# A second chunk in seven products instead of sixteen plain steps, with the weight rounding taken off GpSimd

## The chip, the cores and the metric

The kernel runs on one core of a Trainium2 chip. The metric is the device time of one execution in microseconds (us). A core has engines that run side by side, each with its own queue that it works through in order: TensorE (PE in the profile, with PEld for its weight loads), VectorE (DVE), ScalarE (ACT), GpSimd (POOL) and SyncE (SP), which issues most transfers. An engine stops at an instruction whose operands are not there yet, and everything behind it in its queue stops with it.

## The reference

Retention attention over 8 batches, 8 heads, 576 positions and 64 dimensions is followed by a feed-forward layer on 4608 tokens. All is in 32-bit floats.

```
scores = (q @ k^T) / 8 * gamma_h ** (i - j) for i >= j, else 0
x      = (scores @ v), heads side by side            # 4608 x 512
h      = x @ w_in                                    # 512 -> 2048
g      = h * erf(softplus(h))
out    = g @ w_out                                   # 2048 -> 512
```

The two weights arrive as 64-bit floats, so the kernel has to round them to 32 bits itself, from the two 32-bit words of each number.

## The kernel before

The tokens are cut into 9 chunks of 512 (number c), the 2048 inner features into 4 groups (number g). A `First(g, c)` makes the inner features of one group for one chunk, a `Second` multiplies them by w_out and adds to the output. Both are done as a two-by-two block product by Winograd's scheme: seven block products instead of eight, for which sums of the operands' blocks (and of the results) are made by VectorE. Only the first two chunks of the first group use a plain product with all eight blocks, because at that point the sums are not there.

Attention runs in pieces of 128 tokens, 36 in all, four to a chunk. Each piece has three stages. The text calls them T (bring q and k into transposed form), S (scores, with the mask multiplied in by VectorE) and O (outputs, scaled by VectorE into the x of the chunk, and the running state), each with the piece's number, so that O7 ends chunk 1. They are worked off in one fixed order, and every call of `attend` puts the next of them among the feed-forward work.

```python
    ps_at = ctx.enter_context(tc.tile_pool(name="ps_at", bufs=4, space=PSUM))   # attention's banks
    ps_a = ctx.enter_context(tc.tile_pool(name="ps_a", bufs=2, space=PSUM))
    ps_e = ctx.enter_context(tc.tile_pool(name="ps_e", bufs=1, space=PSUM))     # tags "e" and "g"
    ...
    # order of stages: T0 S0, then T(i+1) O(i) S(i+1); for i = 5 and 7: O(i) T(i+1) S(i+1)
    # from piece 8 on T has its q (from piece 12 on its k too) transposed by VectorE, in 32x32 squares
```

Rounding of one part of a weight (each group has four parts of w_in, "wa", and four of w_out, "wb") takes five steps, and each call of `round_weights(n)` puts n steps in the queues. After a group's last part the sums of its blocks follow as four more steps for wa and four for wb. They overwrite block A21 of w_in, which the plain product reads.

```python
            nc.scalar.activation(a_f, high_f, AF.Abs)                    # step 1, ScalarE
            nc.scalar.mul(out=r_f, in_=low, mul=2.0**-52)
            yield
            nc.vector.tensor_scalar(out=a_f, ... op0=ALU.max, op1=ALU.min)            # step 2
            yield
            nc.vector.tensor_scalar(out=a, ... logical_shift_left, bitwise_and)       # step 3
            yield
            nc.vector.scalar_tensor_tensor(out=a, in0=high, ...)                      # step 4
            yield
            nc.vector.tensor_scalar(out=high, in0=a, scalar1=0xFF800000, ... bitwise_and)   # step 5
            engine = nc.vector if (name, g) == ("wa", 0) else nc.gpsimd
            engine.tensor_tensor(out=r_f, in0=high_f, in1=r_f, op=ALU.mult)
            engine.tensor_tensor(out=a_f, in0=a_f, in1=r_f, op=ALU.add)
            ...
            for n in sums:
                of = (sums_in if n == "wa" else sums_out)(*(operands(n, g)[:, i] for i in range(7)))
                ...
```

The operand sums of x, made by VectorE, and the plain and the seven-product form of `First`:

```python
    def operands_x(g, c):
        ...
        if g == 0 or c < PLAIN:
            tt(t1, b12, b11, ALU.subtract)
            tt(t2, b22, t1, ALU.subtract)
            tt(b12, b22, b12, ALU.subtract)
        else:                      # what was stored in x holds b22 - b12 already
            tt(t2, b12, b11, ALU.add)
            tt(t1, b22, t2, ALU.subtract)
        if g == 0:
            store_x(c)
        tt(t4, b21, t2, ALU.subtract)

        def plain(self):           # 16 steps of two matmuls of 256 columns
            for dc in range(n_dc):
                for n in range(4):
                    for j in range(GP):
                        nc.tensor.matmul(acc[n][...], lhsT=wa[...], rhs=t[:, dc, ...], ...)
                    if dc == n_dc - 1:
                        nc.scalar.copy(out=(self.t2 if tok else self.t1)[:, f], in_=acc[n])
                    yield

        # first(), middle(), last(): 7 steps, each one block product of four matmuls of 256 columns
        def first(self):
            self.product(A11, self.a, True);  nc.scalar.copy(out=self.t1[:, 0], in_=self.a);  yield
            self.product(A12, e, True);  tt(self.t1[:, 0], e, self.t1[:, 0], ALU.add);  yield
        def middle(self):
            self.product(S2, self.a, False);  nc.scalar.copy(out=self.t1[:, 1], in_=self.a);  yield
            self.product(S3, self.e, True);  yield
            self.product(S1, self.a, False);  nc.scalar.copy(out=self.t2[:, 1], in_=self.a)
            tt(self.t2[:, 1], self.e, self.t2[:, 1], ALU.add);  yield
        def last(self):
            self.product(S4, self.a, False);  nc.scalar.copy(out=self.t2[:, 0], in_=self.a);  yield
            self.product(A22, self.e, False);  tt(self.t1[:, 1], self.e, self.t1[:, 1], ALU.add)
            self.softplus();  yield
```

`multiply` forms g from h and erf; `sums` makes the operand sums of the second product, s1 and s2 (part 0), s3 and s4 (part 1). `Second.first` is the products B11 and B21, `Second.middle` T2, T3 and T1, and `Second.last` B22 and T4. T2 is added into the bank of B11, so it has to wait until ScalarE has copied B11 out of it.

The second chunk before, with the first `Second` behind it:

```python
    most[0] = before_chunk(3)
    attend(after_chunk(1))                    # O7
    store_x(1)
    for step, _ in enumerate(firsts[1].plain()):
        if step % 2 == 0:
            attend(min(done[0] + 1, most[0]))
        round_weights(int(step > 1))
        if step == 1:
            firsts[0].softplus()
            firsts[0].erf()
        elif step == 5:
            firsts[0].multiply()
        elif step == 8:
            firsts[0].sums()
    seconds[0].begin()
    run(seconds[0].first(), (2, 2))           # an attend and two rounding steps after each product
    firsts[1].softplus()
```

## Time and profile before

| | before |
|---|---|
| time, median of 3 runs | 1024.89 us (1024.43 to 1025.56) |
| span of the profiled execution | 1024.3 us |
| granted TensorE clock | 1.000 |
| DMA, mean | 162 GB/s |

The page of the profile lists for each engine its busy time and its share of the span, then groups of instructions with their mean duration in ns and the idle time ahead of them. A timeline lists instructions in order of their start, with the duration of the whole row behind the start; several alike are one row (x4). In this trace one matmul of the program is two rows[...], and eight such rows make one block product. Durations of TensorE overlap, so what an instruction really takes of the engine is read from one start to the next.

### The profile page before, as it was taken

What the parts mean: (1) busy time and instruction counts of PE and PEld (TensorE: products, weight loads), DVE (VectorE), ACT (ScalarE), POOL (GpSimd) and SP (SyncE); (2) the same over time, 40 slices, a digit from 0 to 9 for tenths busy, and PEclk for the clock granted to TensorE, in tenths of its full rate; (3) what the DMA queues carried; (4) which work ended last, traced back from release to release, by engine and by line L of the source; (5) the groups of instructions that cost most, each with busy time, mean ns of one, the idle gap of its engine ahead of it and who ended that gap; (6) DMA issues with size and microseconds to landing.
All of it is one profiled execution on the core that took longest, in us unless ns stands there. A gap on an engine that the chain in (4) does not pass through costs nothing.

```text
span 1024.3 us, 15955 instructions
## 1 busy us (share of the span) xinstructions
PE 1014.0 (99%) x6348; PEld 876.5 (86%) x6348; DVE 666.9 (65%) x1062; ACT 390.2 (38%) x481; POOL 122.0 (12%) x122
## 2 busy tenths in 40 slices
PE   8999999999999999999999999999999999999998
PEld 7788888887888888888888888888888888888887
DVE  3769777967976656656666666666567655555555
ACT  2354134233234444434343444444433333333332
POOL 2133112122312110010001001000100000000000
PEclk9999999999999999999999999999999999999999
DMA  9997989969974344544445345444433334444434
GB/s 189 214 245 163 238 194 224 251 152 253 246 188 164 110 159 145 166 160 156 163 142 164 123 147 162 165 144 144 144 124 124 123 131 127 131 136 131 126 88 119
DMA packets 146986, 165.76 MB, mean 162 GB/s; under 512 B 97376, under 2 KB 121568, under 8 KB 138848
## 3 DMA queue, kind: packets, MB, share of 16 engines
q1 hardware_dynamic: 144832, 163.57, 56.1%
q10 hardware_dynamic: 2080, 1.18, 0.5%
q8 instruction: 50, 0.82, 0.3%
q14 instruction: 24, 0.20, 0.1%
HBM read 117.52 MB, written 47.19 MB: 161 GB/s over the span
## 4 chain that ended last, share of the span: by engine, by line
PE 87%; DMA 5%; SPq 3%; DVE 2%; issue 1%; POOL 1%; ACT 0%; ACTq 0%; DVEq 0%; POOLq 0%
PE a L604 23%; PE a L496 22%; PE g L604 12%; PE g L496 11%; PE e L496 6%; PE e L604 5%; PE s L347 2%; PE o L365 2%; DMA wraw<-in_moe_w_in_dram 2%; SPq L147 2%; SPq L131 1%; PE o L388 1%; DMA raw_qs<-in_q_dram 1%; PE o L377 1%; DMA raw_ks<-in_k_dram 1%
## 5 line engine op out<-in xcount | busy, mean ns | idle before, releaser
L496 PE MATMUL a<-x,wa 128*128 128x256 f32 x1088 | 258.3, 380 | 0.0
L496 PEld LDWEIGHTS a<-x,wa 128*128 128x128 f32 x1088 | 205.7, 190 | 28.9 <-issue 0.7
L604 PE MATMUL a<-wb,s 128*128 128x256 f32 x840 | 200.0, 381 | 0.0
L604 PEld LDWEIGHTS a<-wb,s 128*128 128x128 f32 x840 | 158.4, 190 | 23.3 <-ACT o L618 0.7
L99 DVE TENSOR_TENSOR t<-g,t 128x512 f32<-128x512 f32 x68 | 46.9, 690 | 150.1 <-ACT t L526 112.6
L496 PE MATMUL g<-x,wa 128*128 128x256 f32 x544 | 129.2, 380 | 0.0
L496 PEld LDWEIGHTS g<-x,wa 128*128 128x128 f32 x544 | 102.8, 190 | 14.5 <-issue 0.2
L99 DVE TENSOR_TENSOR o<-a,o 128x512 f32<-128x512 f32 x104 | 71.5, 687 | 46.4 <-PE a L604 46.4
L521 ACT COPY t<-a 128x512 f32<-128x512 f32 x34 | 19.9, 586 | 187.8 <-PE a L496 187.8
L99 DVE TENSOR_TENSOR t<-t,s 128x1024 f32<-128x1024 f32 x72 | 88.6, 1271 | 0.0
L565 ACT ACTIVATE s<-t 128x1024 f32<-128x1024 f32 x72 | 72.1, 1048 | 29.6 <-DVE t L99 29.6
L274 POOL TENSOR_TENSOR wraw<-wraw 128x512 f32<-128x512 f32 x28 | 29.5, 1053 | 438.9 <-DVE wraw L272 178.4
L99 DVE TENSOR_TENSOR x<-x 128x512 f32<-128x512 f32 x115 | 75.7, 692 | 1.2
L532 ACT COPY t<-a 128x512 f32<-128x512 f32 x34 | 19.9, 587 | 144.0 <-PE a L496 144.0
L569 ACT ACTIVATE s<-s 128x1024 f32<-128x1024 f32 x72 | 72.1, 1048 | 0.4
L604 PE MATMUL g<-wb,s 128*128 128x256 f32 x280 | 66.7, 381 | 0.5 <-DVE t L99 0.5
L604 PE MATMUL e<-wb,t 128*128 128x256 f32 x280 | 66.6, 380 | 0.0
L604 PE MATMUL a<-wb,t 128*128 128x256 f32 x280 | 66.6, 380 | 0.0
L604 PE MATMUL g<-wb,t 128*128 128x256 f32 x280 | 66.4, 380 | 0.0
L496 PE MATMUL e<-x,wa 128*128 128x256 f32 x272 | 64.8, 381 | 0.0
L99 DVE TENSOR_TENSOR sT<-s,cst 128x512 f32<-128x512 f32 x72 | 46.2, 682 | 25.2 <-PE s L347 25.1
L99 DVE TENSOR_TENSOR o<-g,o 128x512 f32<-128x512 f32 x70 | 48.0, 685 | 21.3 <-ACT o L618 18.6
(86 smaller groups left out, 1245.4 us busy)
## 6 DMA issues: line engine op xcount, KB each, us to landing
od<-o SPq DMA_DIRECT2D x54, 512.0 KB, 3.3
x<-xd SPq DMA_DIRECT2D x27, 1024.0 KB, 4.8
o<-od SPq DMA_DIRECT2D x27, 1024.0 KB, 5.3
raw_qs<-in_q_dram SPq DMA_DIRECT2D x96, 112.0 KB, 4.5
raw_ks<-in_k_dram SPq DMA_DIRECT2D x84, 112.0 KB, 4.2
xd<-x SPq DMA_DIRECT2D x9, 1024.0 KB, 5.1
raw_v<-in_v_dram SPq DMA_DIRECT2D x64, 128.0 KB, 4.4
wraw<-in_moe_w_in_dram SPq DMA_DIRECT2D x32, 256.0 KB, 5.7
```

What stands on the lines that cost most here:

```text
L99: nc.vector.tensor_tensor(out=out, in0=in0, in1=in1, op=op)
L131: nc.sync.dma_start(out=t[part * SQ : (part + 1) * SQ, :, at : at + m - SQ], in_=tokens[:, :, d0 : d0 + m - SQ])
L147: queue.dma_start(out=t[r0 : r0 + n, e::2, :], in_=heads.rearrange("h p d -> p h d"))
L274: engine.tensor_tensor(out=r_f, in0=high_f, in1=r_f, op=ALU.mult)
L347: nc.tensor.matmul(ps[e][:, p, :], lhsT=t["kT"][heads[e], p, :], rhs=t["qT"][heads[e], p, :], start=True, stop=True)
L365: nc.tensor.matmul(o[p % 2][heads[(e + p) % 2], p // 2, :], lhsT=t["v"][:, 2 * p + e, :], rhs=t["sT"][:, e, p, :], start=(p < 2), stop=(no ...
L496: nc.tensor.matmul(acc[:, j * TH : (j + 1) * TH], lhsT=weights["wa", self.g][:, a, d, j * P : (j + 1) * P], rhs=x[self.g, self.c][a][:, d, :],
L521: nc.scalar.copy(out=self.t1[:, 1], in_=self.a)
L532: nc.scalar.copy(out=self.t2[:, 0], in_=self.a)
L565: nc.scalar.activation(self.s[:, j], t, AF.Softplus)
L569: nc.scalar.activation(self.s[:, j], self.s[:, j], AF.Erf)
L604: nc.tensor.matmul(acc[:, tp, :], lhsT=left[:, j * TH + tp * P : j * TH + (tp + 1) * P], rhs=weights["wb", self.g][:, b, j, :], start=(sta ...
```

## The change

The second chunk (c = 1) of the first group is made with seven block products too. That needs the sums of w_in before it (they move ahead of the rounding of w_out, into the first chunk's plain steps, at a point where the last plain read of A21 has been issued) and the operand sums of x for chunk 1. All of w_out's first group is rounded on VectorE, so that GpSimd has no part in it. The sums of the first chunk's activations are split in two. As chunk 1 is now stored with b22 - b12 in it, later groups take the shorter form of `operands_x` for it.

```diff
-                yield src, "wa", g, a, dc % 2, ["wa"] if g > 0 and dc == n_dc - 1 else []
+                yield src, "wa", g, a, dc % 2, ["wa"] if dc == n_dc - 1 else []
 ...
-                    sums = (["wb"] if g > 0 else ["wb", "wa"]) if (f, j) == (1, GP - 1) else []
+                    sums = ["wb"] if (f, j) == (1, GP - 1) else []
 ...
-            engine = nc.vector if (name, g) == ("wa", 0) else nc.gpsimd
+            engine = nc.vector if g == 0 else nc.gpsimd
 ...
-    PLAIN = 2
+    PLAIN = 1
 ...
-    for what in "alkakakawkakakawwaa3awa2aaa5ppppaa5wwppa5ppawappwcppa5ppaaapp5s":
+    for what in "alkakakawkakakawwaa3awa2aaa5ppppaa5wwppa5ppawappwcpp4a5ppaaapp5s":
 ...
     most[0] = before_chunk(3)
     attend(after_chunk(1))
-    store_x(1)
-    for step, _ in enumerate(firsts[1].plain()):
-        if step % 2 == 0:
+    attend(done[0] + 1)
+    operands_x(0, 1)
+    f = firsts[1]
+    for step, _ in enumerate(chain(f.first(), f.middle(), f.last())):
+        if step > 0:
             attend(min(done[0] + 1, most[0]))
-        round_weights(int(step > 1))
-        if step == 1:
+        round_weights((0, 2, 2, 2, 4, 2, 2)[step])
+        if step == 0:
             firsts[0].softplus()
             firsts[0].erf()
+        elif step == 2:
+            firsts[0].multiply()
         elif step == 5:
-            firsts[0].multiply()
-        elif step == 8:
-            firsts[0].sums()
+            firsts[0].sums((0,))
     seconds[0].begin()
-    run(seconds[0].first(), (2, 2))
-    firsts[1].softplus()
+    for step, _ in enumerate(seconds[0].first()):
+        attend(min(done[0] + 1, most[0]))
+        if step == 0:
+            firsts[0].sums((1,))
```

In the string of the first chunk, `a` is one attention stage, `p` one plain step, `w` the load of one weight part, and a digit that many rounding steps.

## The prediction

> **What bounds the kernel now.** I read the page's first part, then busy time by stretches, then the timelines of the four engines between 46 and 110 us (the change lies there), and the chain of work that ended last for the same stretch. The page first, and four stretches (start:end, length, busy time and instructions of PE, PEld, DVE, ACT and POOL, granted clock, DMA share, GB/s):
>
> ```profile
> PE 1014.0 (99%) x6348; PEld 876.5 (86%) x6348; DVE 666.9 (65%) x1062; ACT 390.2 (38%) x481; POOL 122.0 (12%) x122
> 60.88:84.00 23.12, 22.93 (x208) 18.70 (x205) 17.74 (x34) 12.28 (x16) 8.41 (x8) 1.00 0.97 232
> 84.00:99.34 15.34, 15.25 (x157) 12.48 (x155) 13.46 (x20) 9.41 (x11) 4.72 (x5) 1.00 0.82 182
> ...
> 300.00:400.00 100.00, 100.00 (x560) 86.51 (x559) 65.45 (x105) 45.02 (x59) 12.94 (x12) 1.00 0.46 158
> 400.00:500.00 100.00, 100.00 (x465) 88.04 (x464) 63.91 (x99) 42.70 (x52) 9.94 (x9) 1.00 0.43 147
> ```
>
> TensorE is the bound nearly everywhere: without a gap from 300 us on, and with 0.28 us of gaps between 60.88 and 99.34, which is the stretch that the change rewrites. So there is almost no waiting to take away there, and the gain must come from fewer matmuls. But VectorE is busy 31.2 of those 38.5 us, and the change gives it more. Its timeline where the chunk begins, and ScalarE's beside it (start, duration, line and operation, in brackets the idle time ahead and what ended it):
>
> ```profile
> 60.10 0.43 DVE L259 TENSOR_SCALAR wb<-wb 128x512 f32<-128x512 f32 x1 [1.85 <-ACT wb L254]
> 61.75 0.43 DVE L272 TENSOR_SCALAR wraw<-wb 128x512 uint32<-128x512 uint32 x1
> 62.09 0.42 DVE L99 TENSOR_TENSOR sums<-o,state 128x256 f32<-128x256 f32 x1
> 63.09 0.76 DVE L326 STREAM_TRANSPOSE qT<-raw_qs 128x256 f32<-128x256 f32 x2
> 65.54 1.29 DVE L99 TENSOR_TENSOR sT<-s,cst 128x512 f32<-128x512 f32 x2 [1.69 <-PE s L347]
> 70.34 0.43 DVE L259 TENSOR_SCALAR wb<-wb 128x512 f32<-128x512 f32 x1 [3.51 <-ACT wb L254]
> ```
>
> ```profile
> 63.14 1.28 ACT L565 ACT_TABLE_LOAD   x1
> 64.43 2.00 ACT L565 ACTIVATE s<-t 128x1024 f32<-128x1024 f32 x2
> 66.45 1.28 ACT L569 ACT_TABLE_LOAD   x1
> 67.75 2.00 ACT L569 ACTIVATE s<-s 128x1024 f32<-128x1024 f32 x2
> 69.66 0.66 ACT L254 ACTIVATE wb<-wraw 128x512 f32<-128x512 f32 x1
> ```
>
> VectorE has room until 70.34 (3.51 us of it waiting for ScalarE, which is in softplus and erf), and none after. The one real wait in the stretch is in the chain (start, us, what):
>
> ```profile
> 82.98 1.04 POOL wraw L274
> ...
> 84.10 1.62 POOL wb L275
> ...
> 85.74 1.51 DVE wb L99
> ```
>
> GpSimd's add took 1.62 us, VectorE stood still 1.18 us for it, the mask of S10 came late, and O10 lost about 0.4 us on TensorE. That is what the second part of the change is aimed at.
>
> [...]the trace has 690. In a row of independent ones the next starts 0.60 us after the last, in a dependent row 0.72. [...]here multiply 1.05 and add 1.28 to 1.62 against 0.69. [...]the first sum of chunk 0 took 1.77 us beside a GpSimd add, where the others took 0.68. [...]below I count the queues in program order.
>
> **The change part by part.** Three durations carry it: a block product (eight rows) 1.73 us from start to start, a plain step (four rows) 0.865, and 0.1 us more at each passage between attention and a product.
>
> TensorE: 16 plain steps (13.84) become 7 products (12.11): 1.73 us less, the whole direct gain. The number of attention stages is the same.
>
> VectorE, added: eight tensor_tensor for the multiply and add of four parts of w_out, 8 x 0.69 = 5.5; the operand sums of chunk 1, 4 in about 2.85; three adds of the product, 3 x 0.6 = 1.8. Sum 10.1 us. Taken away in the busy part: the four sums of w_in (3.46 from 90.21 to 95.15, where GpSimd slowed them), which now fall at 47.7 to 50.4, into a wait of 3.29 us ahead of the mask at 50.99, and so are free. The parts of w_out that come earliest are free too: part 0 ends about 55.7, ahead of O6 at 55.95. In g = 1 to 3 one tensor_tensor less each, 2 us in stretches where TensorE sets the pace: nothing.
>
> Now the walk through the queues, which decides.
>
> (a) w_out's part 1 is 1.53 us longer on VectorE (62.09 becomes 63.62), so T8's transposes end at 65.4 instead of 63.85. TensorE has O7 to 60.88, T8 to 61.37, A11 to 63.10, A12 to 64.83, then S8, which waits for T8 until 65.5: 0.7 lost.
>
> (b) The operand sums start at 65.3; the second, t2, is there at about 67.05. TensorE is through S8 at 66.6: 0.45 lost. Then S2, T9, S3 to 71.1, O8 (masks at 70) to 72.75, S1 to 74.6, S9, S4 and T10 to 77.95.
>
> (c) ScalarE's A11 copy ends at 63.85, then softplus and erf with their tables take 6.52 as before, so w_out's part 2 can go on at 71.05 on VectorE, behind a wait of 1.1. From there VectorE has, in order: clamp 0.35, T9 0.62, shift and merge 1.08, multiply of chunk 0 2.27, O8 0.66, rest of part 2 1.87, the add of S1 0.6, masks of S9 1.2, part 3 3.5, T10 0.62, two sums of w_out 1.32, s1 and s2 1.32, the add of A22 0.6. The S1 add is thus done at 78.5, the A22 add at 87.0. A22 accumulates in the bank which the S1 add reads: 78.6 instead of 77.95, 0.65 lost.
>
> (d) TensorE goes on: A22 to 80.4, O9 to 81.95, B11 to 83.8, S10 (T10 at 83.9, 0.2 lost), B21 to 86.95. T11's bank comes free with O9's scaling at 88.1: 1.2 lost.
>
> (e) ScalarE's softplus of chunk 1 stands ahead of the copy of B11 and cannot start before the A22 add, 87.0. Two activations of 1.05 each and the copy give 89.8; T2, waiting for that copy, starts there instead of 88.65: 1.15 lost.
>
> (f) From T2 on TensorE sets the pace again: T2 1.82, O10 2.08, T3 1.92, S11 1.09, T1 1.92, O11 2.08. The third chunk's first product starts at 100.7. Before, it started at 99.34.
>
> So 1.73 us of matmuls and about 0.6 of old waits are saved, and about 4.3 us of new waits come in (0.7 + 0.45 + 0.65 + 0.2 + 1.2 + 1.15): with passages that fall otherwise, **+1.4 us** at that point. Behind it VectorE has its sums of chunk 2 at about 105.5 and the masks of S12 at 107.2, where O12 wants them at 107.3, so nothing more is lost, and nothing is won back in a stretch without gaps.
>
> **The rivals.** First: VectorE is quicker than I count, because GpSimd no longer reads beside it (8.41 us of GpSimd work in 60.88 to 84.00, of which 5.2 were the rounding). For it speak the 1.77 and the 1.51 us of slowed instructions; against it, that I took undisturbed durations already. If the waits of (c) to (e) shrink by 3 us, 1.73 + 0.6 less 1.3 makes the kernel 1.0 us faster, 1023.9. Second: the backlog of VectorE is worse. GpSimd still weighs the values (1.04 each) beside the long run of (c), and each collision costs up to a microsecond, through (d) and (e) straight onto TensorE: 1.5 us more, 1027.8. Third: the shift is swallowed later, as at 232 to 252 us, where TensorE waits 1.0 and 0.5 us for transposed k behind transfers. But the chain there goes back through SyncE's queue to a VectorE instruction at 199.06 which itself followed a TensorE product at 196.48, so it moves with the rest; at most a microsecond either way.
>
> **Range and chances.** 1024.89 + 1.4 = 1026.3. As the first rival is the likelier error, I take **1026.0**. The three runs before lie 1.1 us apart, the walk may be off by 1.5, so **1023.8 to 1027.7**. Two per cent are 20 us, more than all the work of the second chunk's product: chances 0.01 faster, **0.98 within 2%**, 0.01 slower.
>
> **What would show it right or wrong.** Right: PE has eight instructions fewer; the four sums of wa lie between 47 and 51 us; no GpSimd multiply or add of wb; TensorE waits at S8, S2, A22, T11 and T2 with VectorE or ScalarE as releaser, some 4 us in all between 60 and 92; the first product of the third chunk starts near 100.7. Wrong: if it starts before 98.5, VectorE kept up and the gain of the matmuls came through; if after 102, there is a wait that I did not see, most likely behind ScalarE's softplus; and if it starts near 100.7 but the time differs from 1026 by over a microsecond, the later DMA stretch around 200 to 250 us swallowed or added time.

## The result, and the profile after

The changed kernel takes 1029.15 us (median of 6 runs, 1027.46 to 1030.04), and the kernel before, in 6 runs beside it, 1024.96 (1024.43 to 1025.94): a ratio of 1.0037, 95% interval 1.0024 to 1.0050. So it is about 4 us slower, where 1.1 was forecast. Two later sets gave 1.0044 [1.0031, 1.0056] and 1.0036 [1.0023, 1.0049].

First the page's line of busy times of the changed kernel, then the same two stretches as before (start:end, length, busy time and rows of PE, PEld, DVE, ACT and POOL, granted clock, DMA share, GB/s):

```profile
PE 1014.1 (99%) x6340; PEld 875.7 (85%) x6340; DVE 674.5 (66%) x1074; ACT 389.8 (38%) x481; POOL 113.0 (11%) x114
```

```profile
60.88:84.00 23.12, 20.93 (x185) 17.10 (x183) 22.29 (x38) 13.94 (x18) 3.95 (x4) 1.00 0.95 218
84.00:99.34 15.34, 13.41 (x114) 10.28 (x113) 10.84 (x22) 6.84 (x8) 1.61 (x2) 0.89 0.77 170
```

PE has the eight rows fewer that seven products instead of 16 plain steps leave out. But in the two stretches it now stands still 2.19 + 1.93 = 4.12 us, where it stood still 0.28, and VectorE is busy 22.29 of the first 23.12 us. The clock column of the second stretch, 0.89, was 1.00 before.

TensorE's rows of the changed kernel that had to wait, with what ended each wait in brackets, and the third chunk's first product:

```profile
64.88 1.16 PE L347 MATMUL s<-qT,kT 64*128 64x128 f32 x16 [0.53 <-DVE qT L326]
66.51 1.96 PE L496 MATMUL a<-x,wa 128*128 128x256 f32 x8 [0.47 <-DVE x L100]
...
78.86 1.99 PE L496 MATMUL g<-x,wa 128*128 128x256 f32 x8 [1.20 <-DVE t L100]
...
88.05 0.63 PE L332 MATMUL pt_k<-ident,raw_k 128*128 128x128 f32 x4 [0.76 <-PE e L604]
89.85 3.38 PE L604 MATMUL a<-wb,s 128*128 128x256 f32 x8 [1.17 <-ACT o L618]
...
102.52 1.99 PE L496 MATMUL a<-x,wa 128*128 128x256 f32 x8
```

The five with waits are S8, S2, A22, T11 and T2, in this order. The waits add up to 4.13 us. (T11's line names TensorE itself as what ended the wait, which tells nothing; it starts at 88.05, inside VectorE's scaling of O9 at 87.54 to 88.28, which frees its bank; in e3, where that ends at 85.4, T11 does not wait.) Two things were not in the forecast: A22 waits 1.20 us, and T2's eight rows, 1.99 us elsewhere, take 3.38. The engines behind A22's wait, in one timeline of GpSimd and VectorE:

```profile
72.40 1.06 POOL L313 TENSOR_TENSOR raw_v<-raw_v,cst 128x512 f32<-128x512 f32 x1 [4.54 <-DMA raw_v<-in_v_dram]
72.48 3.20 DVE L100 TENSOR_TENSOR t<-t,s 128x1024 f32<-128x1024 f32 x2
...
78.12 0.68 DVE L100 TENSOR_TENSOR t<-g,t 128x512 f32<-128x512 f32 x1
```

The multiply of chunk 0 began 0.08 us after GpSimd began to weigh values, and took 3.20 us. The same two instructions in the kernel before, from the timelines of the two engines:

```profile
72.34 2.35 DVE L99 TENSOR_TENSOR t<-t,s 128x1024 f32<-128x1024 f32 x2
...
85.67 1.04 POOL L313 TENSOR_TENSOR raw_v<-raw_v,cst 128x512 f32<-128x512 f32 x1
```

The multiply stood at the same place and took 2.35 us; the weighing came 13 us later, because it stood behind the rounding of w_out's last two parts in GpSimd's queue (75.83 to 85.7): its values had landed at 72.29, and GpSimd stood still for 4.62 us ahead of the last part's multiply (82.98), but the weighing did not pass it. With the rounding gone from that queue, the weighing starts at 72.40, 0.16 us after its values have landed (72.24), and meets the multiply. Everything behind the multiply in VectorE's queue is 0.85 us later, so the add of S1, which frees A22's bank, is too. Behind T2 stands ScalarE, in its own timeline:

```profile
87.32 2.01 ACT L565 ACTIVATE s<-t 128x1024 f32<-128x1024 f32 x2 [7.68 <-DVE t L100]
89.23 0.56 ACT L618 COPY o<-a 128x512 f32<-128x512 f32 x1
```

ScalarE waits 7.68 us for the add of A22 (86.61 to 87.3), does the softplus, and only then the copy that T2 needs. The clock in four stretches of a microsecond (columns as above):

```profile
90.00:91.00 1.00, 1.00 (x4) 0.80 (x5) 1.00 (x3) 0.29 (x1) 0.00 (x0) 0.65 1.18 209
91.00:92.00 1.00, 1.00 (x4) 0.82 (x3) 1.00 (x3) 0.00 (x0) 0.00 (x0) 0.50 0.85 161
92.00:93.00 1.00, 1.00 (x3) 0.42 (x2) 1.00 (x2) 0.00 (x0) 0.00 (x0) 0.50 0.00 0
93.00:94.00 1.00, 1.00 (x11) 0.84 (x12) 0.10 (x1) 0.72 (x2) 0.00 (x0) 0.64 0.00 0
```

Just behind the two waits of T11 and T2 the clock falls to half, from 90.3 to 93.7. A second traced execution of the same kernel has the same two waits and no such fall:

```profile
89.12 0.63 PE L332 MATMUL pt_k<-ident,raw_k 128*128 128x128 f32 x4 [0.76 <-PE e L604]
90.92 1.99 PE L604 MATMUL a<-wb,s 128*128 128x256 f32 x8 [1.17 <-ACT o L618]
```

So I compare executions by two lengths, both from the start of O7 (58.2 to 59.2 us here, ahead of the changed code): to the third chunk's first product, and to the end of VectorE's transposes of q in T13, the last stage that the change was seen to shift on that engine. Before, they are 40.55 and 47.7 us.

| | to third chunk's first product | to T13's q | waits S8 / S2 / A22 / T11 / T2 |
|---|---|---|---|
| before, two traces | 40.55, 40.56 | 47.7, 47.7 | |
| changed, first trace (clock fell) | 44.36 | 52.1 | .53 / .47 / 1.20 / .76 / 1.17 |
| changed, second trace | 42.73 | 50.5 | .53 / .46 / 1.20 / .76 / 1.17 |
| changed, third trace | 42.73 | 50.5 | .53 / .47 / 1.19 / .76 / 1.18 |

Without the fall the change loses 2.2 us to the third chunk's first product; with it 3.8. From there to T13 it loses 0.6 more in either case.

### The profile page after: what moved, and what is told of

Its sections match the earlier page's. It is cut to its first block, busy times and chain, and to the rows that moved or that the text cites. A ratio compares the mean times of both kernels' runs of the same rounds, so it can differ in the third digit from the quotient of the medians.

```text
span 1027.1 us, 15943 instructions
## 1 busy us (share of the span) xinstructions
PE 1014.1 (99%) x6340; PEld 875.7 (85%) x6340; DVE 674.5 (66%) x1074; ACT 389.8 (38%) x481; POOL 113.0 (11%) x114
## 3 DMA queue, kind: packets, MB, share of 16 engines
q10 hardware_dynamic: 2080, 1.18, 0.5%
## 4 chain that ended last, share of the span: by engine, by line
PE 88%; DMA 5%; DVE 4%; ACT 1%; SPq 1%; issue 1%; POOL 0%; DVEq 0%; POOLq 0%
PE a L604 23%; PE a L496 22%; PE g L496 11%; PE g L604 11%; PE e L604 6%; PE e L496 5%; PE o L365 2%; PE s L347 2%; DMA raw_v<-in_v_dram 1%; PE o L388 1%; PE o L377 1%; DMA raw_qs<-in_q_dram 1%; DMA raw_ks<-in_k_dram 1%; DVE t L100 1%; PE f L668 1%
## 5 line engine op out<-in xcount | busy, mean ns | idle before, releaser
L496 PE MATMUL a<-x,wa 128*128 128x256 f32 x1120 | 266.1, 380 | 0.5 <-DVE x L100 0.5
L496 PEld LDWEIGHTS a<-x,wa 128*128 128x128 f32 x1120 | 211.5, 190 | 30.4 <-issue 1.3
L496 PE MATMUL g<-x,wa 128*128 128x256 f32 x560 | 133.1, 380 | 1.2 <-DVE t L100 1.2
L496 PEld LDWEIGHTS g<-x,wa 128*128 128x128 f32 x560 | 105.7, 190 | 16.3 <-DVE t L100 1.4
L100 DVE TENSOR_TENSOR o<-a,o 128x512 f32<-128x512 f32 x104 | 71.4, 686 | 47.7 <-PE a L604 47.7
L274 POOL TENSOR_TENSOR wraw<-wraw 128x512 f32<-128x512 f32 x24 | 25.3, 1053 | 417.0 <-DVE wraw L272 174.1
```

Source lines behind the costliest of these rows:

```text
L100: nc.vector.tensor_tensor(out=out, in0=in0, in1=in1, op=op)
L496: nc.tensor.matmul(acc[:, j * TH : (j + 1) * TH], lhsT=weights["wa", self.g][:, a, d, j * P : (j + 1) * P], rhs=x[self.g, self.c][a][:, d, :],
```

## The experiments

All times are medians, each beside runs of the kernel before in its own set; "d" is the difference of the two medians. "Shift 1" and "shift 2" are the two lengths of the traced execution less 40.55 and 47.7. "Clock" counts the runs whose mean clock was 0.998 or lower, which is what one fall to half for 3.4 us makes of it, wherever it is (the changed kernel's first trace, with one, has 0.998); of the 151 runs of the kernel before in the later sets it was 6.

| run | n | us | d | ratio, 95% | clock | shift 1 | shift 2 |
|---|---|---|---|---|---|---|---|
| changed | 6 | 1029.15 | 4.2 | 1.0037 [1.0024, 1.0050] | 3 of 6 | 3.8 | 4.4 |
| after_again | 5 | 1030.20 | 4.2 | 1.0044 [1.0031, 1.0056] | 1 of 5 | 2.2 | 2.8 |
| after_third | 5 | 1029.42 | 3.4 | 1.0036 [1.0023, 1.0049] | 1 of 5 | 2.2 | 2.8 |
| before_again | 13 | 1025.61 | -0.4 | 0.9997 [0.9989, 1.0005] | 0 of 13 | 0.0 | 0.0 |
| e1_gpsimd | 10 | 1029.08 | 3.1 | 1.0034 [1.0023, 1.0045] | 6 of 10 | 1.6 | 2.1 |
| e2_softplus_later | 6 | 1028.43 | 2.5 | 1.0030 [1.0018, 1.0042] | 1 of 6 | 0.5 | 1.1 |
| e3_sums_later | 8 | 1029.06 | 3.1 | 1.0029 [1.0019, 1.0038] | 1 of 8 | 1.2 | 1.8 |
| e4_dummies | 8 | 1028.98 | 3.0 | 1.0031 [1.0021, 1.0041] | 0 of 8 | 2.2 | 2.8 |
| e5_before_vector | 21 | 1027.08 | 1.0 | 1.0008 [1.0001, 1.0015] | 0 of 21 | 0.8 | 0.8 |
| e6_best | 17 | 1028.15 | 2.1 | 1.0022 [1.0014, 1.0029] | 4 of 17 | 1.1 | 1.1 |
| e9_order | 9 | 1027.76 | 1.4 | 1.0020 [1.0010, 1.0029] | 4 of 9 | 1.4 | 2.0 |
| e11_early_t10 | 13 | 1026.40 | 0.3 | 0.9999 [0.9991, 1.0007] | 2 of 13 | -0.5 | -0.5 |
| e12_after_t10 | 20 | 1028.45 | 2.4 | 1.0025 [1.0018, 1.0032] | 3 of 20 | 1.1 | 1.8 |
| e13_after_t11 | 5 | 1030.66 | 4.9 | 1.0051 [1.0039, 1.0063] | 1 of 5 | 3.5 | 4.1 |
| e14_order_t11 | 22 | 1027.75 | 2.0 | 1.0019 [1.0011, 1.0027] | 14 of 22 | 2.0 | 2.0 |
| e15_before_t11 | 16 | 1027.81 | 2.0 | 1.0022 [1.0015, 1.0030] | 3 of 16 | 1.8 | 1.9 |

Three more (e7, e8, e10, near the end) are 27 to 30 us slower for another reason and not in the table.

### One part undone at a time: e1 to e4

e1 gives w_out's rounding back to GpSimd (w_in's stays on VectorE):

```diff
-            engine = nc.vector if g == 0 else nc.gpsimd
+            engine = nc.vector if (name, g) == ("wa", 0) else nc.gpsimd
```

> The changed kernel with the multiply and add of w_out's first group on GpSimd again; all else as changed. In the changed kernel VectorE carries an unbroken queue from 70.5 us to the add of A22 at 87.2, and TensorE waits 0.5 (S8), 0.5 (S2), 1.2 (A22), 0.8 (T11) and 1.2 us (T2) for it, after which the clock is granted at half for 3.4 us. Theory (the backlog of VectorE makes the waits, and the waits bring the clock down): eight instructions of 0.69 leave VectorE, of which 5.6 us in all and 4 us behind 59 us; S8's wait goes, A22's add comes about 1.5 to 2.5 us earlier, T11 and T2 wait under 1 us together, the clock stays at 1.00, and the kernel is 2 to 4 us faster than the changed one (1025 to 1027). Rival (GpSimd's own lateness and its contention take the place, as the 1.18 us wait for its add in the kernel before): VectorE waits 1 us or more for GpSimd ahead of the sums of w_out, A22's add stays near 87, the clock falls as well, and the time stays at 1028 to 1030.

Measured 1029.08, d 3.1 where the changed kernel has 3.4 to 4.2; the intervals overlap, so a gain of this undoing is not shown. The waits moved: S2 0.34, T11 1.78, T2 1.17, and none at A22. The multiply, the weighing behind GpSimd's rounding, and VectorE's wait, from the timelines of the two engines:

```profile
72.28 2.35 DVE L100 TENSOR_TENSOR t<-t,s 128x1024 f32<-128x1024 f32 x2
...
81.38 1.61 POOL L275 TENSOR_TENSOR wb<-wb,wraw 128x512 f32<-128x512 f32 x1
82.95 1.04 POOL L313 TENSOR_TENSOR raw_v<-raw_v,cst 128x512 f32<-128x512 f32 x1
83.02 1.51 DVE L100 TENSOR_TENSOR wb<-wb 128x512 f32<-128x512 f32 x1 [1.18 <-POOL wb L275]
```

With the rounding back on GpSimd the weighing is late again (82.95), and the multiply takes its 2.35 us. But VectorE waits 1.18 us for GpSimd again, and its clamp at 77.34, 0.42 us alone, takes 1.12 beside GpSimd's add at 76.89.

e2 takes the softplus of chunk 1 off the way of B11's copy:

```diff
-            self.softplus()                       # in last()
+            if (self.g, self.c) != (0, 1):
+                self.softplus()
 ...
+    firsts[1].softplus()                          # behind both products of seconds[0].first()
```

> The changed kernel with chunk 1's softplus put behind B11 and B21, as it was before the change, so that ScalarE copies B11 out of its bank without waiting for the add of A22. Theory: T2 no longer waits 1.17 us for that copy and starts at about 88.6 instead of 89.85; TensorE's pause is then 0.8 us in all, the clock stays at 1.00 or falls for less, and the kernel gains 1.2 us of wait plus 1.7 us of half clock: 1026 to 1027. Rival (the backlog of VectorE is what ends each wait): T2's other operand, the second sum of w_out and s2 at 86.7, is there anyway, but O10 then waits for the masks of S10 at 90.6, so that at most 0.5 us is won and the clock falls as before: 1028.5 to 1029.5.

T2's wait is gone, and shift 1 falls from 2.2 to 0.5. Not all of that is the edit's: in this trace the values landed later, the weighing began 1.5 us behind the multiply, and the collision went the other way. The multiply took 2.35 us, GpSimd's weighing 1.78 instead of 1.04, and A22 waited 0.53, 0.67 less than in the changed kernel. That is close to the 0.65 of the forecast, so it was the collision that made it 1.20. The time, d 2.5, is 0.9 to 1.7 us below that of the changed kernel, but the intervals overlap.

e3 moves the first two sums of activations, and two of w_out's, behind the add of A22 and the scaling of O9:

```diff
-        round_weights((0, 2, 2, 2, 4, 2, 2)[step])
+        round_weights((0, 2, 2, 2, 4, 0, 2)[step])
 ...
-        elif step == 5:
+        elif step == 6:
             firsts[0].sums((0,))
+            round_weights(2)
```

> The changed kernel with two of w_out's four sums and the sums s1 and s2 (2.6 us of VectorE) put behind A22's add and O9's scaling instead of ahead of them; the same instructions in another order. Theory: A22's add ends at about 84.7 instead of 87.3, softplus and the copy of B11 at 87.3 instead of 89.8, T11's bank is free at 85.7 so T11 doesn't wait; T2 then waits for s2, at about 88.3, for under 1 us. The clock stays at 1.00 and the kernel is 2.5 to 3.5 us faster than the changed one: about 1026. Rival (total work of VectorE, not its order, sets the pace): the masks of S10 still come at 90.6, O10 starts no earlier than that, and all but 0.5 to 1 us of the gain is given back there.

A22's add ends at 84.4 instead of 87.3, and T2 waits 0.69 instead of 1.17; A22 still waits 1.19 (the multiply collides here too, 3.20). Shift 1 is 1.2.

e4 fills the waits of T11 and T2 with matmuls nobody reads, and changes nothing else:

```diff
+        if step == 1:
+            idle = ps_e.tile([P, W], FP32, tag="g", name="idle2")
+            keep_busy(4)                          # ahead of T11
         attend(min(done[0] + 1, most[0]))
 ...
+    keep_busy(5)                                  # ahead of T2
```

> The changed kernel with nine matmuls of 128 columns whose result nobody uses put into TensorE's two waits, four ahead of T11 and five ahead of T2; no other engine's work changes. They take the place of waiting only. Theory (T2's eight rows took 3.38 us instead of 1.99 because the granted clock fell to 0.50 from 90.3 to 93.7, and it fell because TensorE had stood still for most of the 3 us before): with the waits filled T2 starts at 89.85 as before, takes 1.9 us, the clock stays at 1.00 throughout, and the kernel is 1.5 to 1.8 us faster than the changed one: about 1027.4. Rival (T2 is slow for another reason, its operands or the transfers of that moment): T2 still takes over 3 us, the clock still shows 0.50, and the time is unchanged or longer by what the nine matmuls take.

TensorE's timeline of e4:

```profile
87.27 1.16 PE L737 MATMUL idle<-ones 128*128 128x128 f32 x8
...
88.70 1.28 PE L737 MATMUL idle<-ones 128*128 128x128 f32 x10
89.81 1.96 PE L604 MATMUL a<-wb,s 128*128 128x256 f32 x8
```

T2 starts at 89.81, as in the changed kernel, and takes 1.96 us. The clock stays at 1.000 in 8 of 8 runs, where 5 of the changed kernel's 16 have 0.998 or lower. By itself that is weak, as its other 11 runs have no such fall and two of its three traces have T2 at 1.99 us; what the fall depends on comes out of the traces further down. In time, d 3.0 against 3.4 to 4.2, the difference is not resolved. Nor do the changed kernel's own runs separate clearly: 11 with a mean clock above 0.998 have a median of 1029.4, the other 5 1029.8.

### The rounding alone: e5

The kernel before, with w_out of the first group on VectorE and the second chunk plain as it was:

```diff
-            engine = nc.vector if (name, g) == ("wa", 0) else nc.gpsimd
+            engine = nc.vector if g == 0 else nc.gpsimd
```

> The kernel before, with the second chunk in plain steps, and all of w_out's first group rounded by VectorE: that part of the change alone. Theory (VectorE has room in the plain chunk but not in the seven-product one): the 1.18 us wait of VectorE for GpSimd's add ahead of w_out's sums goes, and the 0.4 us that O10 lost with it; S8 is later by the 1.5 us of part 1 and TensorE waits up to 0.9 us there. Sum within 0.7 us of the kernel before, either way. Rival (the rounding on VectorE is what costs in the changed kernel): 2 us or more slower, with VectorE as the releaser of TensorE's waits between 60 and 100 us.

It is about 1 us slower, 1.0008 [1.0001, 1.0015]. The stop of VectorE behind GpSimd's add and the loss at O10 are gone, but TensorE's third plain step now waits for O7's x, which VectorE scales behind the rounding (TensorE's timeline):

```profile
64.83 1.10 PE L550 MATMUL pe<-x,wa 128*128 128x256 f32 x4 [1.53 <-DVE x L99]
```

So that part of the change costs by itself what step (a) of the forecast described, and more than it brings. The weighing came forward here too, to 73.56, 1.2 us behind the start of the multiply; it took 2.02 us, and the multiply 2.35.

### A better order: e6, e9, e11, e12

All three of e6, e9 and e11 keep the seven products, move the softplus as e2 does, give the second part of w_out back to GpSimd, and put other pieces of VectorE's queue first.

```diff
 # e6: multiply at step 4, end of the fourth part behind T10, O10 ahead of T2;
 # w_out's sums and all sums of activations in seconds[0].first()
-        round_weights((0, 2, 2, 2, 4, 2, 2)[step])
+        round_weights((0, 2, 2, 2, 2, 2, 0)[step])
 # e9: multiply at step 4; s1 and s2 behind the add of A22 and the scaling of O9,
 # the other sums behind the masks of S10
+        round_weights((0, 2, 2, 2, 4, 2, 0)[step])
 # e11: T10 ahead of the multiply and of the fourth part; multiply at step 5;
 # masks of S10 and O10 ahead of T2; softplus of chunk 1 behind B21
+        round_weights((0, 2, 2, 2, 0, 4, 0)[step])
 ...
+        round_weights(2)                          # in seconds[0].first()
+        firsts[0].sums((step,))
 # e12: the changed kernel, T10 ahead of the fourth part, and with it two of w_out's
 # sums behind the add of A22
+        round_weights((0, 2, 2, 2, 0, 4, 4)[step])
```

> The changed kernel with VectorE's queue rearranged: chunk 1's softplus behind B11 and B21; the multiply of chunk 0 behind the add of S1; w_out's sums and s1, s2 behind A22's add, O9 and the masks of S10; O10 ahead of T2; the second part of w_out on GpSimd. The work is the same. Theory (the order in VectorE's and ScalarE's queues makes the waits): S8, S2, A22, T11 and T2 wait under 1.5 us in all, the clock stays at 1.00, the stretch from O7 to the third chunk's first product falls from 44.4 to 39.5 to 40.5, and the kernel is 3.5 to 5 us faster than the changed one and up to 1 us faster than the kernel before. Rival (something outside this stretch costs the variants 2 us or more): the trace shows the short stretch, and the time still stays 2 us or more above the kernel before.

e6 shortens the run of VectorE ahead of A22, but now T2 waits 0.60 us and the product after it 1.73 for VectorE's sums of activations. Shift 1 1.1, d 2.1.

> The changed kernel with VectorE's queue put in another order than in the first attempt: softplus of chunk 1 behind B21, multiply behind the add of S1, s1 and s2 behind O9's scaling, the last two sums of w_out and s3, s4 behind the masks of S10, the second part of w_out on GpSimd. In the first attempt T3 waited 1.7 us for s3 and T2 0.6 for s2, because O10's scaling stood ahead of them. Theory: the stretch from O7 to the third chunk's first product falls to 38.5 to 39.7 us (44.4 and 42.7 in the changed kernel, 40.6 before), the clock stays at 1.00 there, and the time is 0 to 1.5 us below the kernel before if the loads come no later than before, or up to 1 us above it if the waits after 200 us grow. Rival (VectorE's total, not its order): the stretch stays above 41 us.

In e9 it is S10 that waits, for transposes that stand behind the fourth part's rounding. TensorE's timeline:

```profile
84.13 1.72 PE L347 MATMUL s<-qT,kT 64*128 64x128 f32 x16 [2.07 <-DVE qT L326]
85.78 3.06 PE L605 MATMUL e<-wb,t 128*128 128x256 f32 x8
```

One wait of 2.07 us, and the product behind it takes 3.06 us: the clock is 0.50 from 84.6 to 88.0. It led to e11:

> The changed kernel with a third order in VectorE's queue: T10's transposes ahead of the multiply of chunk 0 and of the fourth part of w_out (so its q buffer is free at about 77.5 us instead of 84, and SyncE can go on with the loads of piece 12), softplus of chunk 1 behind, the masks of S10 and O10 ahead of T2, sums in the order in which the products want them, the second part of w_out on GpSimd. Theory (VectorE's order makes the waits in the chunk, and the late release of q buffers makes the later loads late, which the nearly full transfers from 100 to 280 us do not make good): the stretch from O7 to the third chunk's first product is 39.5 to 40.7 us, no fall of the clock, SyncE waits for T10 no longer than in the kernel before, the waits after 200 us are as before (1.5 to 1.9), and the time is within 1 us of the kernel before, below rather than above. Rival (the time between 100 and 280 us has nothing to do with when the buffers of chunk 1 are freed): the stretch is short as well, and the time still 1.5 to 2.5 us above the kernel before, as it was for the variant with softplus put behind, whose stretch was 41.0 and whose median 2.5 above.

The waits of e11 on TensorE, all of them between 62 and 104 us:

```profile
65.99 1.96 PE L496 MATMUL a<-x,wa 128*128 128x256 f32 x8 [0.35 <-DVE x L100]
...
86.42 1.53 PE L365 MATMUL o<-sT,raw_v 128*64 128x128 f32 x15 [0.30 <-issue]
...
89.72 1.96 PE L605 MATMUL a<-wb,s 128*128 128x256 f32 x8 [0.59 <-DVE s L100]
```

1.24 us of waits instead of 4.13, a stretch 0.5 us shorter than that of the kernel before, and 1026.40 us: level with the kernel before (0.9999 [0.9991, 1.0007]) and some 3 us better than the changed kernel beside it. Its multiply starts at 78.38, well behind the weighing (73.72), and takes 2.32 us. What the order did, another order, with one part of w_out back on GpSimd, undid; how much of it that part gives by itself was not tried.

> The changed kernel with four of its rounding steps (the fourth part of w_out) put behind T10's transposes instead of ahead of them, and the sums of w_out two each moved behind; nothing else. T10's q buffer is free about 3.5 us earlier, VectorE's work up to the add of A22 loses the two sums that go behind it, 1.3 us. Theory (late buffers make late loads): the wait of SyncE for T10 falls from 6.2 to under 4 us, T11 and T2 wait 1 us less, and the kernel is 1.5 to 2.5 us faster than the changed one. Rival (only the waits inside the chunk count): 0.5 to 1.3 us faster.

e12 moves T10 forward and two sums back: T11's wait is gone, T2 waits 0.81. Shift 1 is 1.1, d 2.4. That is 1.0 us below after_third, which ran in the same set, with intervals that overlap; e11 is another 2.0 below, with intervals that don't.

### What else follows the chunk: e7, e8, e10, e13 to e15, and repeats

Behind the chunk TensorE has few waits left, most of them for k near 235 us, where it waits for transfers. I suspected that the loads leave late because SyncE's queue, which issues them, stands behind buffers that VectorE and TensorE still read. e7 (changed kernel), e8 (kernel before) and e10 (e9) move the loads of k and v to ScalarE's queue:

```diff
+            queue = nc.scalar if (name, i) == ("k", 0) or (name != "q" and i >= SQUARES) else nc.sync
```

> The changed kernel with attention's loads of k and v in plain rows, from piece 8 on, issued by ScalarE's queue instead of SyncE's; nothing else moves. In the changed kernel SyncE sits waiting for VectorE's transposes of T10 until 85.15 us, 6.2 us, where it waited 3.8 us before, and its queue is nearly full from 100 to 280 us, with TensorE waiting for transposed k at 216, 237 and 275 us (3.2 us in the last trace, 1.2 in the first). Theory (the backlog of VectorE also delays the loads in SyncE's queue, and that delay comes back as waits after 200 us): with a third of the issues off that queue the waits after 200 us fall under 0.5 us in all, no clock falls there, and the kernel lies 1 to 2.5 us below the changed kernel, relative to the kernel before. Rival (the waits after 200 us are the transfers' own time, not the queue's): they stay at 1.5 to 3 us, and the time doesn't move, or grows by what the issues cost ScalarE.

> The kernel before with the same loads on ScalarE's queue. Theory: its waits after 200 us (1.5 and 1.85 us in two traces) fall under 0.5 us, and it is 1 to 1.5 us faster. If these loads were enough to end those waits, the distance between this kernel and the changed one with the same loads shows the second chunk alone: 2.2 us without a fall of the clock, up to 3.8 with it in every execution. Rival (transfers themselves): no change, 0 to +1 us.

> The last two together: the new order in VectorE's queue and k and v on ScalarE's queue. Theory: both gains add, the stretch from O7 to the third chunk's first product is 38.5 to 40 us and the waits after 200 us are under 0.5 us: 1.5 to 3 us faster than the kernel before. Rival: ScalarE's issues delay its copies out of the banks, TensorE waits for them, and the time is no better than with the new order alone.

They took 1056.26, 1054.12 and 1053.27 us, ratios 1.0287 [1.0273, 1.0301], 1.0274 [1.0260, 1.0288] and 1.0266 [1.0252, 1.0280]. In e7 the scores wait for k 2.97 us at 151.0, 5.09 at 183.3, 3.21 at 213.7 and 4.49 at 257.2: the loads now come late themselves. This says nothing on the theory it was meant for.

The next suspect was T11, released late in the changed kernel (VectorE ends its transposes of q at 93.1). e13 (the changed kernel), e14 (e11) and e15 (the kernel before) exchange T11 and S10:

```diff
+    at = stages.index((scores, 10))
+    stages[at : at + 2] = stages[at + 1], stages[at]
```

> The changed kernel with the stages S10 and T11 in the other order, so that VectorE transposes q of piece 11 right behind O9 and the sums of w_out instead of behind s3, s4 and the add of B21 (ends at about 90.3 us instead of 93.2), and its q buffer is free for piece 13 that much earlier. In fourteen traces so far TensorE waits for a transposed k at 232 to 237 us, in every one, and from there to the end it is 791 to 793 us whatever happened before; that moment has followed the end of T11's transposes (90.2 to 94.5) and of T13's (106.4 to 110.3). Theory (the loads behind T11's release set that moment): it comes 1 to 2 us earlier than in the changed kernel, and the time falls by 1 to 2 us although the waits of the second chunk are the same. Rival (it follows the stretch up to the third chunk's first product, by way of T13): the moment and the time stay within 0.5 us.

> The third order of VectorE's queue, level with the kernel before, with T11 ahead of S10 as well: T11's transposes end at about 87 us instead of 90.8. Theory (T11's release): the moment of the wait at 232.8 us comes up to 1.5 us earlier, which is how long TensorE waits there, and the kernel is 0.8 to 2 us faster than the kernel before. Rival (T13, or TensorE itself): no change, within 0.5 us of the kernel before.

> The kernel before with T11 ahead of S10, and nothing else. T11's transposes end at about 85 us instead of 90.3. Theory (T11's release): its wait at 232 us, 1.0 and 0.7 us in two traces, goes, and the time falls by 0.5 to 1.2 us. Rival: within 0.4 us of the kernel before.

T11 then ends at 90.5, 87.0 and 87.3. e13 is not faster for a T11 that ends 3.0 us earlier behind O7 (d 4.9), and its waits behind the chunk are 2.54 us, so an early T11 alone does not end them. In e15 they are 0.60 us, and the one near 232 is gone, as its theory had it; but TensorE also comes there 1.8 us later, and the exchange itself costs 2.0 us. So T11's part in them is not told apart. In e14 S10 waits for VectorE's scaling of O9, and the product behind runs at half clock (TensorE's timeline):

```profile
86.16 1.13 PE L347 MATMUL s<-qT,kT 64*128 64x128 f32 x14 [2.26 <-DVE x L100]
87.21 3.33 PE L607 MATMUL e<-wb,t 128*128 128x256 f32 x8
```

Here the clock does separate the runs: 8 above 0.998 have a median of 1025.9, the other 14 1028.8. So it does in e1: 4 have 1028.1, the other 6 1030.6.

When the clock falls can be worked out from the traces. Its record begins at 4.97 us in the changed kernel's first trace, and the fall at 90.31 comes 25 steps of 3.413 us later. In e9 it is 23 steps (6.06 to 84.56), in e14 24 (5.79 to 87.71), in e6, behind a wait for k, 67 (6.92 to 235.61), in e12, in the start-up, 6 (6.90 to 27.38). One such step each of the changed kernel's first and second trace, and the fullest one of e12 with no fall behind it (columns as above; PE is the first):

```profile
86.90:90.31 3.41, 1.48 (x8) 0.85 (x7) 3.41 (x8) 2.96 (x4) 0.00 (x0) 1.00 1.01 215
89.03:92.44 3.41, 2.15 (x11) 1.79 (x12) 3.41 (x7) 2.32 (x4) 0.00 (x0) 1.00 1.17 211
232.18:235.59 3.41, 1.64 (x11) 1.16 (x11) 1.66 (x3) 1.70 (x3) 0.00 (x0) 1.00 0.95 209
```

In the first TensorE stood still 1.93 us and the clock fell; in the others 1.26 and 1.77, and it did not. Over the 20 traces, up to the last matmul, 19 falls begin at the end of such a step, and TensorE stood still 1.81 us or more in each; of those that end at the full clock with no fall behind them none has more than 1.77. So the same two waits bring the clock down where one step holds both of them, and not where a border lies between them. An estimate from these figures: the waits, 2.56 us from the first's begin to the second's end, lie in one step in about a third of the possible positions; 5 of 16 runs have a mean clock as low as one fall makes it.

Three repeats, without an edit, settle how far two traces or sets of one kernel differ:

> The changed kernel once more, unaltered, beside the kernel before on the same chip. Four variants that took a part of its waits or its half clock away still measured 2.5 to 3.1 us above the kernel before, so it must be seen how far the changed kernel lies above it on this chip. If the new waits of the second chunk and the fall of the clock behind them make the whole difference, the median is again 3.5 to 4.5 us above; the stretch from O7's start to the third chunk's first product, 44.4 us in its trace against 40.6 before, is again 43 to 45. If the difference lies elsewhere (start-up, the transfers between 200 and 260 us), that stretch is near 41 to 42 in the new trace and another one longer.

> The changed kernel unaltered, beside the two above on the same chip, so that the differences above can be taken within one set of runs: 3.5 to 4.5 us above the kernel before, the stretch from O7 to the third chunk's first product 42.7 us without a fall of the clock at T2 and 44.4 with it.

> The kernel before, unaltered, as a measure of what two sets of runs of the same kernel differ by: the interval should hold 1.000 and be about 0.001 wide on either side. Its new trace shows whether the first plain product starts near 30.0 us, as in its first trace, or near 29.3, as in the traces of the changed kernel and its variants (which at that point are the same program).

The kernel before repeats its lengths within 0.02 us, and so does the changed kernel where its clock doesn't fall. The fall is thus extra, and not part of every execution.

The waits of TensorE behind T13 (most for k near 235 and 274 us) differ from trace to trace, and with them the time. A span can be laid out whole: up to O7, from O7 to T13's q, TensorE's waits behind that, and the rest.

| trace | span | to O7 | O7 to T13's q | waits behind | rest |
|---|---|---|---|---|---|
| before | 1024.3 | 58.79 | 47.74 | 1.54 | 916.2 |
| before_again | 1024.6 | 58.68 | 47.75 | 1.85 | 916.3 |
| changed | 1027.1 | 58.16 | 52.13 | 1.19 | 915.6 |
| after_again | 1028.4 | 59.22 | 50.51 | 3.22 | 915.5 |
| after_third | 1027.2 | 58.34 | 50.50 | 2.70 | 915.7 |
| e5_before_vector | 1026.3 | 58.77 | 48.50 | 1.84 | 917.2 |
| e11_early_t10 | 1024.6 | 58.35 | 47.27 | 2.91 | 916.1 |
| e13_after_t11 | 1028.6 | 58.56 | 51.85 | 2.54 | 915.7 |

The means of the changed kernel's three against the two of before: 0.2 us less up to O7, 3.3 more to T13, 0.7 more of waits, 0.7 less in the rest: 3.1 in all. In the two traces without the fall of the clock, 2.8 of O7 to T13 and 1.3 more of waits.

## Why the prediction was off

**The bound and the direction held.** TensorE waits at S8, S2, A22, T11 and T2, 4.13 us against a forecast sum of 4.35. That they are so near is partly luck: the walk to 100.7 holds 37.6 us of work behind O7's start, the trace 38.6 (42.73 less 4.13), so TensorE came later to places where VectorE decides, and waited less there. Without its gaps the stretch was 40.27 us (40.55 less 0.28), so 1.67 went. But 0.5 of that is O10's old loss, which no gap shows (2.60 us from start to start before, 2.09 in e5), so of the matmuls' 1.73 only about 1.2 arrived; B11, B21 and T11, with other neighbours now, each take some 0.2 us longer. The sums of w_in are free: at 46.98, inside VectorE's old wait, though in 4.23 us beside GpSimd and not in 2.7.

**(a), (b)** 0.53 and 0.47 us, forecast 0.7 and 0.45. e5 shows (a)'s cause alone: the same late rounding, with 1.53 us at a plain step.

**(c) failed in one term.** "Multiply of chunk 0 2.27" (from its start to the next) was 3.13, because GpSimd weighed values beside it. A22 waited 1.20, not 0.65, and its add came 0.9 us later behind O7 than I had it. The second rival named this collision and its 1027.8 was nearer; I took the first rival as likelier, although I had noted against it that undisturbed durations were counted already. What I missed is that the collision comes from the change: GpSimd's queue, which I did not walk through, had held the weighing back behind the rounding, until 85.67, and without it the weighing came to 72.40, beside a multiply that stayed where it was. e1 and e5 show it from both sides: with the rounding on GpSimd the weighing is at 82.95, without it, in plain steps, at 73.56. (Of GpSimd's 8.41 us the rounding was 5.8, not 5.2.)

**(d)** S10 did not wait and T11 waited 0.76, not 1.2: TensorE came there 1.0 us later behind O7 than I had it, by A22's longer wait and by longer work, and the scaling of O9 only 0.6.

**(e)** 1.17 us, forecast 1.15, and e2 shows that the softplus ahead of the copy is its cause. But T2 itself is at 31.7 us behind O7, not 31.0, by the multiply's excess of 0.85.

**(f) is the step that failed: "+1.4 us at that point", and "nothing more is lost, and nothing is won back".** It was +2.2 at that point. Of the 0.8 us, 0.7 were there at T2, from (c). The sum in the text doesn't give 1.4 either: 4.35 less 1.73 and 0.6 is 2.0, and the rest was put down to "passages that fall otherwise", which fell the other way. Two more losses came behind:

- The clock. Two waits of 0.76 and 1.17 us let the clock fall for 3.4 us in one of three traces, for 1.6 us more; the first product of the third chunk came at 102.5, in the range "after 102" that I called a wait that I did not see. It was no wait. I hadn't reckoned with a fall of the clock behind waits so short; the traces show the half (0.50), the length (3.41 us), that it comes in some traces of a kernel and not in others, and that 1.81 us of standing still in one step were enough. What the fall adds to the median is left open.
- VectorE's queue again. T12's transposes now stand behind the add of T1 (101.16), and T13's end 7.8 us behind the third chunk's first product instead of 7.2: 0.6 us, in all three traces. I had followed VectorE to the masks of S12 (107.80 in the first trace, where I had 107.2), and no further.

2.2 + 0.6 are 2.8 us without the fall and 4.4 with it, where the forecast has 1.4 and then nothing. The medians are 3.4 to 4.2 us above those of the kernel before; the rest is what comes and goes behind the chunk, and its cause is not shown.

**The third rival** (the shift swallowed or added to at 232 to 252 us, "at most a microsecond either way") was a real term of the sum: the waits behind T13 are 1.2, 3.2 and 2.7 us in the changed kernel's traces and 1.5 and 1.9 before, so from 0.5 us less to 1.5 more than the mean of before. They follow no rule that these runs show: 2.91 us in e11, whose T13 is early, and 2.54 in e13, whose T13 is late. What sets them stays open, T11's part in it too, and whether SyncE's queue does could not be told. Open too is why the rest is 0.5 to 0.8 us shorter in the changed kernel. Because of both, the single shifts of the table of runs foretell d only within about 1.4 us (d less shift 2 is 0.6 us in the mean of the 15 rows other than before_again, from -0.6 to 1.4), though the ends are in order: 0.3 at -0.5, and 4.9 at 4.1.

## What to carry to other kernels

Where an engine has no gap, fewer instructions on it pay only if the engines that feed it keep their order of hand-overs: here 1.7 us of TensorE's work went and 4.1 us of waits came in, and another order (e11, with one part of w_out back on GpSimd) got 3 us back. When an operation is taken off a queue, what stood behind it there comes forward, as the weighing did from 85.67 to 72.40: walk through the relieved queue as well as the loaded one, and look what its next operation will then run beside. Look also at what each hand-over queue puts ahead of the next consumer. Add up the waits of TensorE that lie close together, as here 1.81 us or more of them in one step of 3.41 us brought the clock down, and measure such a change by a length between two events of a trace as well as by the total.

## What the runs showed of the hardware

- The clock of TensorE fell to 0.50 for 3.41 us where TensorE had stood still for 1.81 us or more in one step of a grid of 3.413 us, counted from the begin of the clock's record: 19 falls in 20 traces, none behind a step with 1.77 us or less. The same waits of 0.76 + 1.17 us lay in one step in the changed kernel's first trace (1.93 us), and across a border in the two others (1.26 and 1.52 us at most), where the clock stayed at 1.00.
- In the kernel before, VectorE's tensor_tensor over 512 columns, the 690 ns of the prediction, took 0.69 us where GpSimd did nothing beside it. Chunk 0's s3 and s4, where the second doesn't read the first, start 0.60 us apart (79.56 and 80.16), and the rounding's multiply and add, where it does, 0.73 (40.57 and 41.30). GpSimd's multiply over 512 columns took 1.04 us, its add 1.28 to 1.61.
- Where GpSimd's weighing and VectorE's pair of multiplies ran side by side, one of them or both took longer. In seven traces the weighing began from 0.08 us ahead of the pair of multiplies to 0.85 behind, and the pair took 3.2 us (in the changed kernel's first trace the first of the two 2.07 instead of 1.22), the weighing 1.06 to 1.85. In e5 and e2 it began 1.2 and 1.5 us behind; the pair took its undisturbed 2.35 us, and the weighing 2.02 and 1.78 instead of 1.04. In e1 VectorE's clamp, with one tensor input, took 1.12 us instead of 0.42 beside an add of GpSimd.
- Loads of k and v issued from ScalarE's queue instead of SyncE's made the kernel before 2.7% slower, 1054.12 us against 1026.37 (e8).
